# A Fourier mixing and long convolution kernel: the first transform stage with 64 points, high and low halves in one operand

## The chip, the cores and the metric

The kernel runs on one core of one Trainium2 chip, as one launch. The metric is the device time in microseconds; three runs of the kernel before gave 1201.86, 1202.92 and 1202.91, a median of 1202.91. All other times below are microseconds of one profiled execution, counted from the start of its span, unless they are marked ns.

The engines are called as the profile calls them: PE multiplies matrices (PEld is its loading of the stationary operand), DVE is the vector engine, ACT the scalar engine, POOL the GpSimd engine, and SP issues DMAs. ACT and POOL issue DMAs too.

## The reference

Four layers work on `x`, of 2048 positions (S) by 576 channels (D), all in float32. Layers 1 and 3 are A, layers 2 and 4 are B:

```
A:  n = layernorm(x)
    a = n @ Wre.T ; b = n @ Wim.T            # 576 x 576 cosine and sine matrices
    x = x + Cre @ a - Cim @ b                # 2048 x 2048 cosine and sine matrices
B:  kv = causal_conv4(k, shift_k) * v        # per channel, 4 taps
    y  = irfft(rfft(pad(kv)) * rfft(pad(ssm_k)))[:2048] + kv * ssm_D
    x  = x + layernorm(x) * y
```

B's `y` depends only on inputs, so the kernel computes it once and uses it in both B layers.

## The kernel before, in words

**Numbers.** PE multiplies in a float32 form of reduced precision. Each operand is therefore split into a high part, rounded to that form by an ACT copy, and a low part, the remainder, which DVE subtracts (`split`, line 90). A product of two split operands takes three PE products: high x high, high x low, low x high.

**First layer.** `layer` (line 291) goes through 4 column blocks x 2 matrices (Cre, Cim) x 16 row blocks: 128 steps, n = 0 to 127. A step loads a 128x512 block of C two steps ahead (`load_c`, line 204) and splits it, and issues 12 products of 512 columns into four banks `s` and two into the bank `rm`. The sixteen normed row tiles of `x` are made during the first steps (`get_x0`). At n = 15, 31, 47, ... the banks are copied out and split into `u`. After each second time, the product with W is due: 4 x 2 pieces of 27 products of 288 columns (`hidden`, line 267, bank `bk`), kept in `pending` and issued by `finish`. W (9 chunks of 128x576, split) lies in the region `ra`, which the convolution uses before.

**The branch.** Beside these steps runs the generator `branch` (line 338), which computes `y` as a transform in stages. Position s = 16p + j has p on the partitions and j = 0 to 15 as the row. There are 32 rows: 16 of the kernel `ssm_k` (src 1) and 16 of the signal kv (src 0).

- The first transform stage makes, for each row, a product over p with cosine and sine constants (`fc`, a 128 x 4 x 128 tile, loaded by POOL's queue). `f1_split` splits the row into `xf`; `f1_products` (line 423) issues for each half of the channels and each of two components three products into a bank, copies it out on ACT (`so`) and stores it to DRAM (`t_d`) from ACT's queue. Each `yield` in it ends one half of the channels, here called a group: six products before.
- Signal rows come from `convolve` (line 373), seven DVE operations for each pair of rows (1152 elements on 128 partitions), into the ring `rp` of two pairs in region `ra`, times `v`.
- The middle stage (lines 457 to 607, from `m1`) reads `t_d` back in 64 loads, makes the second transform step, the product of the two spectra, and the first inverse step; the second inverse step (`i2_products`) follows and gives `yb_d`.

**What sets the order.** The loop at line 734 interleaves steps and branch. `used` counts the calls of the branch in the first transform stage (68 at its end); `want` is a function of n and says how many should have been made; it reaches 68 at n = `F1_END` = 42. A product of a row follows its split by one or two rows. From n = `W_FROM` = 41, each half step loads one chunk of W through a ring `wl` of three tiles and splits it. At n = `MID_LOAD` = 44 the middle stage begins to load, and from `MID_FROM` = 47 its work is spread evenly over the planned time up to `I2_END` = 111, so that `spent` follows `passed`. At n = 47 all eight pieces of the first column block are issued ahead of that step's products, with middle work between them. The scheduler that places the instructions keeps each engine's queue in order at run time; `issue_after` places an instruction behind another one of the same engine.

```
want = int(4 + F1_16 * at / 8 if at <= 16 else at16 + (68 - at16) * (at - 16) / (F1_END - 16))
todo = [(1, 1), (0, 1)] + [(j, 1) for j in range(2, K_FIRST)] + [(j, 0) for j in range(K_FIRST)]
todo += [(j, src) for j in range(K_FIRST, J) for src in range(2)]
```

So before, `todo` starts with four kernel rows and four signal rows, and then alternates.

Of the kernel before, what the change touches and what calls it, by code (L numbers as in the profile page):

```python
# [15 lines left out]
P = 128  # L16
# [16 lines left out]
F1_END = 42  # L33
W_FROM = 41
HOLD = 125
W_SAVE = 60
MID_LOAD = 44
MID_FROM = 47
# [26 lines left out]
def fnet_h3_kernel(ctx: ExitStack, tc: tile.TileContext, x, c_mat, w_re, w_im, k_pad, v, shift_k,  # L65
# [126 lines left out]
    t_d = [dr.tile([P, J, 2, 2, HD], F32, name=f"t{h}") for h in range(2)]  # L192
# [22 lines left out]

    def load_w():
        lay(flts, SC_AT + CRAW * NT + 4 * D, ("wl", D, 3))
        wg = region_a(FR, "w").rearrange("p (k n) -> p k n", k=9)
        for ch in range(9):
            w = two(wg[:, ch])  # L220
            raw = ring["wl"]()
            if ch < 8:
                nc.sync.dma_start(raw, (w_re if ch < 4 else w_im)[(ch % 4) * P:(ch % 4 + 1) * P, :])
            else:
                nc.sync.dma_start(raw[:REM], w_re[NC * P:, :])
                nc.sync.dma_start(raw[REM:], w_im[NC * P:, :])
            for lo, hi, sg in ((0, P, 1 if ch < 4 else -1),) if ch < 8 else ((0, REM, 1), (REM, P, -1)):
                if sg > 0:
                    split(w[lo:hi, 0, :], w[lo:hi, 1, :], raw[lo:hi])
                else:  # L230
                    nc.scalar.activation(w[lo:hi, 0, :], raw[lo:hi], AF.Copy, scale=-1.0)
                    nc.vector.scalar_tensor_tensor(w[lo:hi, 1, :], raw[lo:hi], -1.0,  # L232
                                                   w[lo:hi, 0, :].bitcast(F32), op0=OP.mult,
                                                   op1=OP.subtract)
            W.append(w)
            yield
# [101 lines left out]
    def branch():  # L338
        f1r = region_b(FR, "f1r")
# [17 lines left out]
        def load_k(upto):  # L357
            while k_loaded[0] < min(upto, (J + 4) // 2):
# [4 lines left out]
                                          ap=[[J * D, P], [1, 2 * D]]))  # L363
# [26 lines left out]
        todo = [(1, 1), (0, 1)] + [(j, 1) for j in range(2, K_FIRST)] + [(j, 0) for j in range(K_FIRST)]  # L390
        todo += [(j, src) for j in range(K_FIRST, J) for src in range(2)]
        loads = [0]

        def f1_loads(upto):
            while loads[0] < min(upto, len(todo)):
                j, src = todo[loads[0]]
                loads[0] += 1
                if j not in fcs:
                    fcs[j] = quads(ring["fc"]())
# [11 lines left out]
        def f1_split(j, src):  # L411
# [303 lines left out]
    with tc.issue_after(biased[0]):  # L715
# [4 lines left out]
        with behind(rounded[0]):  # L720
            load_c((0, 0, 1))
        load_x(2)
    used = 4
    first_lo = parted[1]
    next(br)
    next(br)
    with behind(first_lo):
# [378 lines left out]
```

## Time and profile before

| what | before |
|---|---|
| median of three runs | 1202.91 |
| profiled execution: its time, its span | 1201.11, 1199.3 |
| PE busy, share of the span | 1180.6, 98% |
| DVE busy, share | 839.9, 70% |
| ACT busy, share | 665.9, 56% |
| granted PE clock | 0.998 |
| first-stage products (`bk<-f1r`) | 384 |

A line of a group of instructions reads: line of the kernel, engine, operation, written tile <- read tiles, shape, xcount | busy time, mean ns of one | idle time of the engine just before, and what ended it. A timeline line begins with the start and the length. Tile names: `f1r` holds `xf` and `fc`, `f1f` the convolution, `mats` the split rows of `x` and blocks of C, `flts` the loaded data, `w` the split W, `t` and `vd` the DRAM tiles between the stages, `mid` the operands of the middle stage. Matmuls overlap, so the mean of one is longer than the distance between two. A table of windows gives for each stretch the busy time of every engine in it with its count of instructions, the granted PE clock, the mean busy share of the 16 DMA engines and what they moved.

### The profile page before, as it was taken

The page shows a single profiled execution, that of the slowest core. Times are in us where ns is not written, and L with a number is a line of the kernel's source. Part 1 is how long each engine was busy: PE and PEld are TensorE (multiplying, and loading weights), DVE is VectorE, ACT ScalarE, POOL GpSimd, SP SyncE. Part 2 cuts the span into 40 slices and gives each one's busy share as a digit, 9 for nine tenths or more (in the row PEclk, how much of TensorE's full clock was granted, in tenths as well). Part 3 has the DMA queues.
Part 4 walks back from the last instruction along what each step waited for, and adds up shares of the span by engine and source line. Part 5 has one row for each costly group of instructions (what it writes and reads, how often), then busy time and mean ns, then how long its engine had stood idle before and what let it go on. Part 6 is the DMA issues. An engine that isn't in the chain of part 4 may idle for free.

```text
span 1199.3 us, 18263 instructions
## 1 busy us (share of the span) xinstructions
PE 1180.6 (98%) x6320; PEld 1026.0 (86%) x6320; DVE 839.9 (70%) x1498; ACT 665.9 (56%) x1335; POOL 75.5 (6%) x116
## 2 busy tenths in 40 slices
PE   7999999999999999999999999999999999999997
PEld 6888888988888888888988898888888888789997
DVE  7899883679777677675447766875676777774674
ACT  8855665679877768675435666544444435450210
POOL 2210000000000000001101121000000000001111
PEclk9999999999999999999999999999999999999999
DMA  9879898546656766658967686872772677794621
GB/s 340 308 226 318 275 304 256 177 133 182 216 177 199 213 180 207 187 149 249 305 202 236 222 257 213 271 264 71 216 281 74 207 275 269 237 347 142 214 96 40
DMA packets 146111, 261.96 MB, mean 218 GB/s; under 512 B 15841, under 2 KB 44769, under 8 KB 146018
## 3 DMA queue, kind: packets, MB, share of 16 engines
q1 hardware_dynamic: 102674, 205.58, 53.6%
q10 hardware_dynamic: 36432, 42.63, 10.3%
q0 software_dynamic: 6912, 12.59, 4.1%
q8 instruction: 49, 0.80, 0.3%
q14 instruction: 44, 0.36, 0.1%
HBM read 194.09 MB, written 66.65 MB: 217 GB/s over the span
## 4 chain that ended last, share of the span: by engine, by line
PE 84%; DVE 6%; DMA 4%; ACT 3%; issue 2%; POOL 1%; SPq 0%; POOLq 0%; DVEq 0%; ACTq 0%
PE s L74 46%; PE bk L74 33%; PE rm L74 5%; DMA flts<-in_c_mat 2%; ACT flts L486 1%; DVE mats L92 1%; DVE f1f L382 1%; DMA flts<-t 1%; POOL flts L616 1%; DVE mats L189 1%; ACT mid L486 1%; DVE f1f L387 0%; DMA t<-flts 0%; DVE u L92 0%; ACT mats L91 0%
## 5 line engine op out<-in xcount | busy, mean ns | idle before, releaser
L74 PE MATMUL s<-mats 128*128 128x512 f32 x2088 | 531.2, 392 | 0.8 <-DVE flts L613 0.3
L74 PEld LDWEIGHTS s<-mats 128*128 128x128 f32 x2088 | 381.1, 188 | 71.1 <-DVE mats L189 1.1
L92 DVE TENSOR_TENSOR mats<-flts,mats 128x512 fp32r<-128x512 f32 x206 | 140.7, 688 | 58.4 <-ACT mats L91 55.7
L91 ACT ACTIVATE mats<-flts 128x512 fp32r<-128x512 f32 x206 | 128.2, 627 | 85.4 <-PE bk L74 30.9
L74 PE MATMUL bk<-mid 128*128 128x288 f32 x768 | 131.1, 300 | 1.8 <-ACT flts L486 0.8
L74 PEld LDWEIGHTS bk<-mid 128*128 128x128 f32 x768 | 114.3, 188 | 21.2 <-ACT flts L486 8.4
L492 DVE TENSOR_TENSOR mid<-flts,mid 128x576 fp32r<-128x576 f32 (+1 forms) x160 | 101.9, 637 | 34.4 <-ACT mid L486 31.3
L74 PE MATMUL bk<-w,u 128*128 128x288 f32 x864 | 121.0, 296 | 0.7 <-DVE w L232 0.5
L74 PEld LDWEIGHTS bk<-w,u 128*128 128x128 f32 x864 | 117.4, 188 | 4.4 <-ACT flts L486 1.1
L486 ACT ACTIVATE flts<-bk 128x288 f32<-128x288 f32 x160 | 61.9, 404 | 87.4 <-PE bk L74 74.0
L74 PE MATMUL rm<-mats 128*128 128x512 f32 x304 | 94.9, 391 | 0.0
L486 ACT ACTIVATE mid<-flts 128x576 fp32r<-128x576 f32 (+1 forms) x159 | 86.8, 582 | 7.5 <-DMA flts<-t 3.7
L486 ACT ACTIVATE flts<-flts 64x288 f32<-64x288 f32 x192 | 85.0, 443 | 5.7
L432 ACT ACTIVATE flts<-bk 128x288 f32<-128x288 f32 x128 | 49.4, 408 | 47.0 <-PE bk L74 46.4
L74 PEld LDWEIGHTS bk<-f1r 128*128 128x128 f32 x384 | 59.5, 191 | 13.8 <-ACT f1r L91 7.4
L74 PE MATMUL bk<-f1r 128*128 128x288 f32 x384 | 64.5, 300 | 6.7 <-ACT f1r L91 6.7
L74 PE MATMUL bk<-mats 128*128 128x288 f32 (+1 forms) x376 | 67.8, 317 | 0.0
L74 PEld LDWEIGHTS rm<-mats 128*128 128x128 f32 x304 | 57.0, 188 | 12.1 <-DVE flts L264 0.3
L74 PE MATMUL s<-t,mats 128*128 128x512 f32 x264 | 64.9, 389 | 0.0
L278 DVE TENSOR_TENSOR flts<-flts,bk 128x288 f32<-128x288 f32 x48 | 21.7, 453 | 61.1 <-PE bk L74 58.8
L175 POOL TENSOR_TENSOR flts<-flts 128x1 f32<-128x1 f32 x35 | 28.9, 827 | 524.2 <-DVE flts L174 524.2
L74 PE MATMUL bk<-mats,t 128*128 128x288 f32 (+1 forms) x368 | 59.3, 303 | 0.0
(143 smaller groups left out, 1491.8 us busy)
## 6 DMA issues: line engine op xcount, KB each, us to landing
flts<-in_c_mat SPq DMA_DIRECT2D x148, 256.0 KB, 3.6
ph<-in_c_mat SPq DMA_DIRECT2D x54, 512.0 KB, 3.9
t<-flts ACTq DMA_DIRECT2D x64, 288.0 KB, 4.6
flts<-t SPq DMA_DIRECT2D x64, 288.0 KB, 2.9
flts<-in_c_mat SPq DMA_DIRECT2D x30, 512.0 KB, 5.3
vd<-flts ACTq DMA_DIRECT2D x64, 144.0 KB, 2.5
flts<-vd SPq DMA_DIRECT2D x32, 288.0 KB, 4.8
mid<-in_i2c POOLq DMA_DIRECT2D x32, 256.0 KB, 5.6
```

What stands on the lines that cost most here:

```text
L74: nc.tensor.matmul(ps, lhsT, rhs, start=first, stop=last, skip_group_check=more)
L91: a = nc.scalar.activation(h, src, AF.Copy).ins
L92: return a, nc.vector.tensor_tensor(l, src, h.bitcast(F32), OP.subtract).ins
L175: pows.append(nc.gpsimd.tensor_tensor(rs, ve, mhalf, OP.pow).ins)
L189: made.append(nc.vector.tensor_tensor(t[:, D + REM:], y[:, :NC * P], h[:, :NC * P], OP.subtract).ins)
L278: added[:] = [nc.vector.tensor_tensor(r[:, cs], r[:, cs], ps[:, :HD], OP.add).ins]
L382: nc.vector.tensor_tensor(out_t[:, n], k, wt[3 - t][:, n], OP.mult)
L432: stored[:] = [nc.scalar.activation(so[:, c, :], ps[:, :HD], AF.Copy).ins]
L486: last_act.append(nc.scalar.activation(*args, **kw).ins)
L492: nc.vector.tensor_tensor(l, src, h.bitcast(F32), OP.subtract)
L616: pows.append(nc.gpsimd.tensor_tensor(rs, sv, mhalf, OP.pow).ins)
```

## The change

The first stage's transform over 128 points becomes one over 64 points; the rows' positions are split by even and odd, and the second step becomes one of 32 points in place of 16 (constants only; the middle stage's instructions stay). The host puts the even half on partitions 0 to 63 and the odd half on 64 to 127. With 64 points, an operand's high part takes 64 partitions and its low part the other 64, so that one product covers both: `xf[0]` holds the even half's high and low parts, `xf[1]` the odd half's. A bank now takes two products (constants' high part, constants' low part), a group four.

To place the parts:
- a kernel row gets two ACT copies on 64 partitions (of the very first row, one is DVE's) and two DVE subtractions on 64 partitions that write the other half of the partitions;
- a signal row gets one ACT copy on 128 partitions, one on 64, one DVE subtraction on 128 in place, and two DMAs from SBUF to SBUF on SP's queue, each of 64 partitions x 576 elements, one call later (`crossing`).

The order `todo` becomes four kernel rows, all sixteen signal rows, then twelve kernel rows (j = 11 to 15, then 10 down to 4); some constants `fc` are loaded a second time. The calls of the branch follow a new curve: 10 at n = 14, 26 at n = 30, 43 at n = 45, and the rest by n = 49, of which 12 during the eight pieces at n = 47. The middle stage begins to load at n = 50 and runs from 53 to 111. The nine chunks of W are copied inside DRAM to `w_d` at n = 22, 24, ... 38, loaded into their final place in region `ra` at n = 45 (four) and 45.5 (five), and split in place at n = 46. At n = 46 one tile each of the rings `so` and `land` is given to the residual loads of `hidden`.

```
-F1_END = 42
-W_FROM = 41
+F1_V = 45
+F1_END = 49
+F1_PIECE = 1.5
+W_RAW = 22
+W_AT = {45: 4, 45.5: 5}
+W_SPLIT = 46
+RES_AT = 46
-MID_LOAD = 44
-MID_FROM = 47
+MID_LOAD = 50
+MID_FROM = 53
...
+    def split_raw(t, ch):
+
+        for lo, hi, sg in ((0, P, 1 if ch < 4 else -1),) if ch < 8 else ((0, REM, 1), (REM, P, -1)):
+            h, l = t[lo:hi, 0, :], t[lo:hi, 1, :]
+            if sg > 0:
+                split_in(h, l)
+            else:
+                raw = l.bitcast(F32)
+                nc.scalar.activation(h, raw, AF.Copy, scale=-1.0)
+                nc.vector.scalar_tensor_tensor(l, raw, -1.0, h.bitcast(F32), op0=OP.mult, op1=OP.subtract)
+
     def load_w():
-        lay(flts, SC_AT + CRAW * NT + 4 * D, ("wl", D, 3))
+        for ch in range(9):
+            if ch < 8:
+                load_after(w_d[ch][:, :D], (w_re if ch < 4 else w_im)[(ch % 4) * P:(ch % 4 + 1) * P, :])
+            else:
+                load_after(w_d[ch][:REM, :D], w_re[NC * P:, :])
+                load_after(w_d[ch][REM:, :D], w_im[NC * P:, :])
+            yield
         wg = region_a(FR, "w").rearrange("p (k n) -> p k n", k=9)
         for ch in range(9):
             w = two(wg[:, ch])
-            raw = ring["wl"]()
...
+            load_after(w[:, 1, :].bitcast(F32), w_d[ch][:, :D])
             W.append(w)
+            yield
+        for ch in range(9):
+            split_raw(W[ch], ch)
             yield
...
-        todo = [(1, 1), (0, 1)] + [(j, 1) for j in range(2, K_FIRST)] + [(j, 0) for j in range(K_FIRST)]
-        todo += [(j, src) for j in range(K_FIRST, J) for src in range(2)]
-        loads = [0]
+        first, last = [1, 0, *range(2, K_FIRST)], [*range(J - 5, J), *range(J - 6, K_FIRST - 1, -1)]
+        todo = [(j, 1) for j in first] + [(j, 0) for j in range(J)] + [(j, 1) for j in last]
+        loads, fc_at, crossing = [0], {}, []
...
             xf = parts("xf")
-            parted[:] = split(xf[0], xf[1], r)
+            if not src:
+                h = [nc.scalar.activation(xf[0], r, AF.Copy).ins, nc.scalar.activation(xf[1][hi], r[hi], AF.Copy).ins]
+                parted[:] = h + [nc.vector.tensor_tensor(r.bitcast(FR), r, xf[0].bitcast(F32), OP.subtract).ins]
+                crossing.extend(((xf[0][hi], r[lo]), (xf[1][lo], r[hi])))
+                return xf
+            sides = (xf[0], lo, hi), (xf[1], hi, lo)
+            if (j, src) == todo[0]:
+                h = [nc.scalar.activation(xf[0][lo], r[lo], AF.Copy).ins, nc.vector.tensor_copy(xf[1][hi], r[hi]).ins]
+            else:
+                h = [nc.scalar.activation(t[at], r[at], AF.Copy).ins for t, at, to in sides]
+            with behind(h[1]):
+                parted[:] = h + [nc.vector.tensor_tensor(t[to], r[at], t[at].bitcast(F32), OP.subtract).ins
+                                 for t, at, to in sides]
             return xf
...
-                for c in range(2):
+                for h in range(2):
                     ps = bank()
-                    mm(ps[:, :HD], fc[:, c, :], xf[0][:, cs], True, False)
-                    mm(ps[:, :HD], fc[:, c, :], xf[1][:, cs], False, False)
-                    mm(ps[:, :HD], fc[:, 2 + c, :], xf[0][:, cs], False, True)
-                    stored[:] = [nc.scalar.activation(so[:, c, :], ps[:, :HD], AF.Copy).ins]
-                nc.scalar.dma_start(t_d[hf][:, j, :, src, :], so)
+                    mm(ps[:, :HD], fc[:, 2 * h, :], xf[h][:, cs], True, False)
+                    mm(ps[:, :HD], fc[:, 2 * h + 1, :], xf[h][:, cs], False, True)
+                    stored[:] = [nc.scalar.activation(so[:, h, :], ps[:, :HD], AF.Copy).ins]
+                nc.scalar.dma_start(t_d[hf][:, :, j, src, :], so)
                 yield
...
             for half in range(2):
+                while half and crossing:
+                    dst, t = crossing.pop(0)
+                    nc.sync.dma_start(dst.bitcast(F32), t)
                 next(products, 0)
...
+    def f1_want(at):
+        return np.interp(at, (0, 14, 16, 30, 32, F1_V, F1_END), (4, 10, 11, 26, 27, 43, 68 - 2 * TB * F1_PIECE))
+
     spent = passed = 0.0
-    total = (I2_END + 1 - MID_FROM) * STEP + 3 * 2 * TB * PIECE
+    pieces = 0
+    total = (I2_END + 1 - MID_FROM) * STEP + 2 * 2 * TB * PIECE
...
+            if whole is None:
+                at, pieces = n - 0.75, pieces + 1
+            want = int(f1_want(at) + pieces * F1_PIECE)
             with behind(made[min(n + 2, J - 1)], *evac):
-                while used < want:
+                while used < min(want, 68):
                     next(br)
                     used += 1
```

More of the change, by code (lines that the diff above doesn't have):

```diff
@@ L1067, in _constants @@
         i1[1, a, :, a, :, 1] = c.T
+    r = np.arange(2 * J)
+    th = 2 * np.pi * (r[:, None] * (r // J + r % J * 2)[None, :] % 32) / 32
+    f2 = np.zeros((2, 2, 2 * J, 2, 2, 2 * J))
+    c, s = np.cos(th), np.sin(th)
+    for a in range(2):
+        f2[a, 0, :, 0, a, :] = c
+        f2[a, 1, :, 0, a, :] = s
+        f2[a, 0, :, 1, a, :] = -s
+        f2[a, 1, :, 1, a, :] = c
     m = [*_parts(f2.reshape(P, P)), *_parts(i1.reshape(P, P))]
```

90 lines of the change are left out of this document (40 added, 50 removed).

## The prediction

> **What bounds the kernel now.** I read the page first (busy shares, then the chain that ended last), next a table of windows cut at the ends of steps, and then the instruction rows of the stages that the change touches. A step is one pass of the first layer over one 128x512 block of the sequence matrix: 12 products into `s` and 2 into `rm`, so every second `rm` product ends a step.
>
> The page's busy line for all engines and its chain by engine:
> ```profile
> PE 1180.6 (98%) x6320; PEld 1026.0 (86%) x6320; DVE 839.9 (70%) x1498; ACT 665.9 (56%) x1335; POOL 75.5 (6%) x116
> PE 84%; DVE 6%; DMA 4%; ACT 3%; issue 2%; POOL 1%; SPq 0%; POOLq 0%; DVEq 0%; ACTq 0%
> ```
> The windows end at steps 0, 16, 42, 46, 52, 64, 79, 111 and at the end. Columns: stretch, length, busy of PE, PEld, DVE, ACT, POOL with instruction counts, granted clock, DMA share, GB/s.
> ```profile
> core 0: us, PE busy (x) PEld busy (x) DVE busy (x) ACT busy (x) POOL busy (x), PEclk, DMA share, GB/s
> 0.00:13.42 13.42, 6.86 (x28) 5.94 (x28) 7.91 (x26) 9.00 (x16) 2.87 (x9) 1.00 0.89 304
> 13.42:74.01 60.59, 60.15 (x282) 49.43 (x282) 53.39 (x120) 50.50 (x104) 15.00 (x17) 1.00 0.86 294
> 74.01:198.99 124.98, 124.80 (x669) 108.36 (x669) 104.39 (x123) 74.05 (x165) 5.28 (x10) 1.00 0.90 284
> 198.99:213.29 14.30, 14.30 (x71) 12.10 (x70) 4.99 (x8) 7.08 (x13) 1.58 (x3) 1.00 1.01 313
> 213.29:281.03 67.74, 66.22 (x417) 59.18 (x416) 51.48 (x102) 49.27 (x107) 0.00 (x0) 1.00 0.50 150
> 281.03:333.85 52.82, 52.82 (x277) 45.70 (x277) 44.59 (x87) 46.42 (x99) 0.00 (x0) 1.00 0.61 191
> 333.85:442.85 109.00, 108.49 (x635) 94.59 (x635) 76.36 (x153) 75.43 (x169) 2.12 (x4) 1.00 0.66 198
> 442.85:622.32 179.47, 178.69 (x1004) 156.58 (x1004) 108.27 (x197) 110.87 (x235) 13.73 (x26) 1.00 0.70 216
> 622.32:1199.30 576.98, 568.23 (x2952) 494.19 (x2951) 388.57 (x690) 243.29 (x433) 34.87 (x48) 1.00 0.63 207
> ```
> PE is busy almost everywhere, at a granted clock of 1.00. Busy can still hide a slow PE, so I take the pace of its products from a stretch in which nothing waits:
> ```profile
> 189.99 1.54 PE L74 MATMUL s<-mats 128*128 128x512 f32 x6
> 191.36 0.96 PE L74 MATMUL bk<-f1r 128*128 128x288 f32 x6
> 192.17 1.55 PE L74 MATMUL s<-mats 128*128 128x512 f32 x6
> ```
> From start to start, six 512-column products take 1.37 (0.228 each, 3.18 for the 14 of a step) and six 288-column products take 0.81 (0.135 each). Window 3 holds 26 steps, that is 364 wide products and 305 narrow ones: 364 x 0.228 + 305 x 0.135 = 124.2 of its 124.98. So PE sets the pace there, and a product that is taken out is time, as long as nothing else becomes the pace.
>
> Much else is nearly there already. In the middle of the first transform stage DVE is never idle and the DMA engines are full:
> ```profile
> 97.12:141.27 44.15, 44.15 (x243) 38.77 (x242) 43.60 (x48) 25.96 (x58) 2.64 (x5) 1.00 1.00 329
> ```
>
> **The change part by part.** *Fewer products.* `f1_products` issued 2 halves x 2 components x 3 products for each of 32 rows, 384 in all; it now issues 2 x 2 x 2, 256. 128 x 0.135 = 17.3 off PE. Shapes, banks (128), evictions (128) and stores to `t` (64) stay the same.
>
> *Start.* The first kernel row is the first thing PE uses:
> ```profile
> 5.82 0.68 ACT L91 ACTIVATE f1r<-flts 128x576 fp32r<-128x576 f32 x1 [0.75 <-DMA flts<-in_ssm_k]
> 6.54 0.76 DVE L92 TENSOR_TENSOR f1r<-flts,f1r 128x576 fp32r<-128x576 f32 x1 [0.56 <-ACT f1r L91]
> ```
> It now needs two subtractions on 64 partitions in place of one on 128, before DVE goes on to the first halves of C. A half costs no less than a whole, as ACT and then DVE rows from steps 56 to 62 show (mean ns after the comma):
> ```profile
> L486 ACT ACTIVATE flts<-flts 64x288 f32<-64x288 f32 x21 | 9.3, 443 | 0.5
> L486 ACT ACTIVATE flts<-bk 128x288 f32<-128x288 f32 x13 | 5.3, 410 | 2.4 <-ACT flts L486 1.8 <-DVE flts L508 0.5
> L506 DVE TENSOR_TENSOR flts<-bk,flts 64x288 f32<-64x288 f32 x7 | 3.2, 460 | 0.2
> L505 DVE TENSOR_TENSOR flts<-bk,flts 128x288 f32<-128x288 f32 x7 | 3.2, 457 | 5.8 <-ACT flts L486 5.8
> ```
> So one more 0.7 in the opening chain; and of the products removed here about four (0.5) only filled a wait. Cost 1.2; bounds 0.5 and 2.
>
> *Steps 1 to 16.* I count from the code which calls of the branch each step makes. Product groups (one call, now four products) done by step 16 fall from 12 to 9, convolution operations from 18 to 13; ACT gains one 64-partition copy for each of three kernel rows and loses three groups' evictions. I book no further cost.
>
> *Steps 17 to 42.* Signal rows come first, so the whole convolution must end by step 40. The calls of these steps hold 26 product groups, 14 signal rows and 43 convolution operations. DVE's pace, start to start:
> ```profile
> 99.45 1.35 DVE L382 TENSOR_TENSOR f1f<-f1f 128x1152 f32<-128x1152 f32 x1
> 100.72 0.68 DVE L92 TENSOR_TENSOR mats<-flts,mats 128x512 fp32r<-128x512 f32 x1
> 101.32 0.75 DVE L92 TENSOR_TENSOR f1r<-flts,f1r 128x576 fp32r<-128x576 f32 x1
> 101.99 1.35 DVE L387 TENSOR_TENSOR f1f<-f1f 128x1152 f32<-128x1152 f32 x1
> ```
> That is 1.27 for a convolution operation, 0.60 for a half of C, 0.67 for a row. DVE: 43 x 1.27 + 26 x 0.60 + 14 x 2 x 0.67 + 3.7 for the eviction at step 31 = 92.7. PE: 26 x 3.18 + 26 x 4 x 0.135 = 96.7. DMA, in MB: a signal row moves 0.295 (v) + 0.262 (its constants) + 0.590 (two stores) + 0.295 (k) + 0.295 (the two new crossing transfers, 64 partitions x 2304 B each) = 1.74; 13.5 rows, 26 blocks of C at 0.262 and the nine new copies of W inside DRAM (2.65) make 32.9 MB. At the 329 GB/s of the row above that is 100.0, more than PE's 96.7; there DMA was at that share and PE still lost nothing, with peaks above the mean. I take 100, a loss of 3.3 against today's 0.8: cost 2.5. Bounds: a gain of 0.8 if all losses go, and 15.6 at the slowest rate that a full stretch shows, 291 GB/s (113.1):
> ```profile
> 90.00:100.00 10.00, 10.00 (x54) 8.40 (x53) 10.00 (x13) 5.72 (x13) 0.53 (x1) 1.00 0.97 291
> ```
> ACT gets a third pass over each signal row (14 x 0.59) and has room: 74.05 of 124.98 today.
>
> *SP.* It gets 32 crossing issues, 9 copies, and 9 loads where there were 10: about 40 more at 0.33 each. They are cheap, but a crossing transfer waits for DVE's subtraction with the next load of C queued behind it. SP already waits so for buffers that a row's split frees (total, times, longest):
> ```profile
> SPq L407 <- DVE f1r L92: 14.5, 9, 4.6
> ```
> C is loaded two steps ahead, some 7.4, against a 4 to 5 landing, so I book nothing; if that cover goes, each late block costs 1 to 2. The convolution's next write of a row pair also has to wait until its crossing transfers have read it; in DVE's order about 7 of other work lies between, against 4 to 5 for issue and landing.
>
> *W.* Before, W came through three buffers from step 41 on, one chunk each half step. Now nine loads (2.65 MB) go out at steps 45 and 45.5 and nine splits (9 x 0.6 on ACT, 9 x 0.7 on DVE) are traced at step 46, ahead of the hidden products of step 47, which need all nine chunks within their first 3.6. SP, which runs about 1.5 steps ahead, issues them some 13 before they are needed. In those 13 also go three blocks of C and about six product groups' stores, loads and constants, 4.2 MB: 6.9 MB at 329 GB/s is 21, so 8 late. Filling PE meanwhile are the remaining product groups, of which 22 (12 us of PE) are traced from step 47 on. I take half, 4. Bounds: 2 better than today (window 5 today loses 1.5 idle, and a little busy), and 10.
>
> *Middle stage.* It starts at step 53 in place of 47 and still ends at 111, without the eight hidden products of step 47 beside it. The planner's total falls from 65 x 3.2 + 24 x 3.6 = 294 to 59 x 3.2 + 16 x 3.6 = 246, so 1.195 times the work in each step. Today a step of 4.38 holds one unit of nine products:
> ```profile
> 295.05:325.48 30.43, 30.43 (x160) 26.23 (x160) 24.07 (x48) 26.04 (x56) 0.00 (x0) 1.00 0.64 202
> ```
> Seven steps, seven units: a unit is about 3.0 of ACT and 2.75 of DVE. After: PE 3.18 + 1.195 x 1.21 = 4.63, ACT 0.6 + 1.195 x 3.0 = 4.2, DVE 3.9. PE stays the longest, with 91% ACT. In steps 65 to 79 (635 products: 210 x 0.228 + 425 x 0.135 = 105.3 of 109.0) 3.7 is lost today; I take 2.3 more over the stage. Bounds 0 and 6.
>
> *Sum*, on the profiled execution (span 1199.3, its time 1201.1): -17.3 + 1.2 + 2.5 + 4 + 2.3 = -7.3, so 1193.8. The median of the runs, 1202.9, lies 1.8 above that execution: 1195.6.
>
> **The rivals.** *The saving arrives almost whole.* For it: PE kept its pace at a DMA share of 1.00 and with DVE full. Then only the start and 1 us elsewhere cost: 1202.9 - 15 = 1188. *DMA becomes the pace of steps 17 to 42.* The crossing transfers are on 64 partitions, and after the first stage such transfers landed no sooner than twice the bytes did (KB each, us to landing, 199 to 218):
> ```profile
> flts<-in_w_im SPq DMA_DIRECT2D x3, 288.0 KB, 4.3
> flts<-in_w_re SPq DMA_DIRECT2D x1, 144.0 KB, 6.0
> ```
> If the 28 crossing transfers of the stage take the engines for twice their bytes, 37.0 MB at 329 GB/s is 112.6, another 12.6: 1208, slower than before. It decides from 107.3 up (100 + 7.3), that is below 307 GB/s for the plain bytes. Against it: that landing includes waiting behind others, and the two of a pair run opposite ways. [...] *W is late by its whole 8 and more*, with ACT's splits holding up the halves of C behind them: at the bound of 10, 1201.6, no change. *The products don't get fewer* is excluded by the code. *ACT sets the middle stage*: at the bound of 6, 1199.3, still faster.
>
> **How the numbers follow.** What can be told from no change here is 0.2%, 2.4 us. Forecast (with the middle stage's case) 0.52, own range 1190 to 1200; saving almost whole 0.18; DMA the pace 0.20, of which slower 0.15 and no change 0.05; W late 0.10, half no change, half slower through both. Faster 0.70, same 0.10, slower 0.20. The range for 8 in 10 leaves out the upper part of the DMA case and the lowest of the first rival: 1187 to 1208.
>
> **What would show it.** 256 products on `f1r`; a first layer in which steps 17 to 42 take about 100, with DMA share near 1.0 and DVE above 90%; waits of `s` products for halves of C if SP or DMA is late; an idle PE just ahead of the first `bk<-w,u` product if W is; ACT about 91% in steps 53 to 64. The prediction is wrong if the 26 steps take over 105, or if PE waits over 8 at step 47.

## The result, and the profile after

The change made the kernel slower: a median of 1230.53 in four runs (1227.2 to 1231.26) against 1202.91, a ratio of 1.0226 (95% interval 1.0206 to 1.0246). The prediction said 1195.6, with a range of 1187 to 1208, and faster. The profiled execution of the changed kernel took 1230.05, with a span of 1228.3 and a mean granted clock of 0.987.

The page of the changed kernel, its busy line, its chain by engine, and the group of the first-stage products:
```profile
PE 1183.6 (96%) x6192; PEld 1018.3 (83%) x6192; DVE 855.3 (70%) x1515; ACT 686.6 (56%) x1366; POOL 76.3 (6%) x123
PE 76%; ACT 7%; DMA 7%; DVE 5%; issue 3%; POOL 0%; ACTq 0%; SPq 0%; POOLq 0%; DVEq 0%
L79 PE MATMUL bk<-f1r 128*128 128x288 f32 x256 | 51.5, 321 | 20.6 <-DVE f1r L447 8.4
```
There are 128 products fewer, as said, and yet PE is busy for 3 longer: busy hides slow products. The chain has less of PE (76% against 84%) and more of ACT, DMA and issue: PE now stands waiting.

The windows of the changed kernel, cut at the ends of the same steps as those of before (0, 16, 42, 46, 52, 64, 79, 111, end), with the same columns:
```profile
0.00:18.02 18.02, 9.02 (x22) 6.44 (x22) 10.11 (x28) 11.00 (x19) 4.44 (x10) 1.00 0.86 295
18.02:80.85 62.83, 58.63 (x255) 47.26 (x256) 53.42 (x120) 50.57 (x102) 10.20 (x15) 0.97 0.78 255
80.85:188.34 107.49, 99.48 (x464) 82.18 (x464) 94.46 (x106) 54.57 (x109) 5.83 (x11) 0.97 0.90 280
188.34:207.06 18.72, 16.90 (x82) 13.58 (x82) 10.45 (x16) 13.76 (x29) 0.00 (x0) 1.00 0.93 301
207.06:282.72 75.66, 68.99 (x397) 62.43 (x397) 30.55 (x46) 40.03 (x85) 5.30 (x10) 0.91 0.69 219
282.72:341.63 58.91, 55.88 (x279) 46.70 (x279) 47.52 (x93) 49.88 (x108) 0.00 (x0) 0.97 0.66 210
341.63:456.58 114.95, 114.66 (x676) 100.15 (x676) 92.27 (x186) 90.26 (x205) 0.54 (x1) 1.00 0.64 192
456.58:651.08 194.50, 191.19 (x1076) 165.66 (x1075) 127.58 (x236) 132.67 (x283) 15.37 (x29) 1.00 0.74 225
651.08:1228.30 577.22, 568.88 (x2952) 493.85 (x2951) 388.91 (x690) 243.84 (x433) 34.66 (x48) 0.99 0.63 207
```
The last row is 577.2 long, against 577.0 before, so nearly the whole difference lies in steps 0 to 111 of the first layer, which end at 651.08 against 622.32: 28.8 later.

To see where, I take from the length of each stretch the time that its products need at PE's pace: 0.227 for one of 512 columns (14 in a step) and 0.1345 for one of 288 (the rows of the kernel before from 189.99 to 192.17 give 0.228 and 0.135). What is left I call PE's loss. Steps 17 to 42 of the changed kernel hold 364 + 100 products: 107.5 - 82.6 - 13.5 = 11.4 (11.7 with the products counted step by step, as in the table). "e1" is the first experiment below.

| steps | loss before | loss after | difference | the prediction's term | loss in e1 |
|---|---|---|---|---|---|
| 0 | 8.6 | 13.8 | +5.2 | +1.2 (start) | 13.2 |
| 1 to 16 | 2.1 | 8.0 | +5.9 | 0 | 6.3 |
| 17 to 42 | 1.7 | 11.7 | +10.0 | +2.5 | 2.3 |
| 43 to 52 | 4.4 | 17.4 | +13.0 | +4 (W) | 15.0 |
| 53 to 111 | 7.9 | 19.7 | +11.8 | +2.3 (middle stage) | 20.3 |
| sum | 24.7 | 70.6 | +45.9 | +10.0 | 57.1 |
| products at the pace | 597.5 | 580.2 | -17.3 | -17.3 | 580.2 |

So the 17.3 came, and 45.9 of losses came with it, in every stage. The loss of steps 17 to 42 isn't spread out: 8.8 of it is in step 32, 0.9 in steps 17 to 31 and 2.0 after. Step 16 alone lost 4.3. After steps 15 and 31 the banks `s` are copied out; rows of the timeline of the changed kernel around step 32 (start, length, ..., idle time before and its releaser):
```profile
128.71 0.75 DVE L438 TENSOR_TENSOR f1f<-f1f,f1r 128x576 fp32r<-128x576 f32 x1
129.38 1.35 DVE L395 TENSOR_TENSOR f1f<-f1f 128x1152 f32<-128x1152 f32 x1
129.52 1.12 SPq L476 DMA_DIRECT2D f1r<-f1f  x2
...
136.73 2.63 DVE L395 TENSOR_TENSOR f1f<-f1f 128x1152 f32<-128x1152 f32 x2 [3.33 <-DMA f1r<-f1f]
...
143.08 2.48 DVE L97 TENSOR_TENSOR u<-s,u 128x512 fp32r<-128x512 f32 x4
143.82 4.61 PE L79 MATMUL s<-mats 128*128 128x512 f32 x12 [6.31 <-DVE u L97]
```
A signal row's subtraction (L438) ends at 129.46. Its two crossing transfers are issued from 129.52 on, the second at 130.09. The convolution wants to write that row of the ring again at 133.40; it has to wait until 136.73, 6.6 after the second issue. In DVE's queue stand behind it the rest of the convolution's work and then the four subtractions that free the banks: PE waits 6.31 for the first. And when it goes on, its 12 products take 4.61, where a row of 12 takes 2.9 at the full clock (2.88 at 80.69 in the same trace). The next rows, of windows 3.4 long, say why (after the stretch its length and PE's busy time; the third number from the end is the clock):
```profile
137.00:140.40 3.40, 0.51 (x4) 0.27 (x3) 3.40 (x4) 2.37 (x5) 0.00 (x0) 1.00 0.42 138
140.40:143.80 3.40, 0.00 (x0) 0.00 (x0) 3.40 (x5) 0.00 (x0) 0.00 (x0) 0.51 0.83 253
143.80:147.20 3.40, 3.38 (x8) 2.71 (x9) 3.31 (x6) 0.86 (x2) 0.00 (x0) 0.50 0.00 1
```
In the second and the third of them the granted clock is half, 0.51 and 0.50.

The convolution waited so four times, as the table of waits of the changed kernel has it (engine, line, waited for: sum, times, longest), and this one of them stood ahead of PE's banks:
```profile
DVE f1f L395 <- DMA f1r<-f1f: 7.4, 4, 3.3
```

### The profile page after: what moved, and what is told of

Read it like the earlier page. It is cut to its first block, busy times and chain, and to the rows that moved or that the text cites. A ratio compares the mean times of both kernels' runs of the same rounds, so it can differ in the third digit from the quotient of the medians.

```text
span 1228.3 us, 18204 instructions
## 1 busy us (share of the span) xinstructions
PE 1183.6 (96%) x6192; PEld 1018.3 (83%) x6192; DVE 855.3 (70%) x1515; ACT 686.6 (56%) x1366; POOL 76.3 (6%) x123
## 4 chain that ended last, share of the span: by engine, by line
PE 76%; ACT 7%; DMA 7%; DVE 5%; issue 3%; POOL 0%; ACTq 0%; SPq 0%; POOLq 0%; DVEq 0%
PE s L79 43%; PE bk L79 29%; PE rm L79 4%; ACT flts L515 3%; DMA f1r<-f1f 2%; ACT mid L515 1%; DMA flts<-t 1%; DMA t<-flts 1%; DMA flts<-vd 1%; DVE mats L97 1%; ACT mats L96 1%; DVE mid L521 1%; DMA t<-ud 1%; DMA vd<-flts 0%; DVE f1f L395 0%
## 5 line engine op out<-in xcount | busy, mean ns | idle before, releaser
L79 PE MATMUL s<-mats 128*128 128x512 f32 x2088 | 538.9, 396 | 10.0 <-DVE u L97 7.1
L79 PEld LDWEIGHTS s<-mats 128*128 128x128 f32 x2088 | 387.1, 190 | 85.1 <-DVE u L97 8.8
L79 PE MATMUL bk<-mid 128*128 128x288 f32 x768 | 135.1, 303 | 5.7 <-ACT mid L517 2.2
L521 DVE TENSOR_TENSOR mid<-flts,mid 128x576 fp32r<-128x576 f32 (+1 forms) x160 | 102.0, 638 | 35.1 <-ACT mid L515 25.7
L515 ACT ACTIVATE flts<-bk 128x288 f32<-128x288 f32 x160 | 61.2, 402 | 67.1 <-PE bk L79 55.1
L79 PE MATMUL bk<-f1r 128*128 128x288 f32 x256 | 51.5, 321 | 20.6 <-DVE f1r L447 8.4
L459 ACT ACTIVATE flts<-bk 128x288 f32<-128x288 f32 x128 | 46.2, 406 | 44.2 <-PE bk L79 38.7
L79 PEld LDWEIGHTS bk<-f1r 128*128 128x128 f32 x256 | 42.7, 201 | 31.0 <-ACT flts L459 9.6
```

Of the source, the lines that this page charges most:

```text
L79: nc.tensor.matmul(ps, lhsT, rhs, start=first, stop=last, skip_group_check=more)
L459: stored[:] = [nc.scalar.activation(so[:, h, :], ps[:, :HD], AF.Copy).ins]
L515: last_act.append(nc.scalar.activation(*args, **kw).ins)
L521: nc.vector.tensor_tensor(l, src, h.bitcast(F32), OP.subtract)
```

## The experiments

A ratio is to the kernel before on the same chip (medians of before there: 1201.0 to 1202.2), with its 95% interval.

**The crossing by ACT, not by DMA (e1_act_cross).** Undoes the two transfers of a signal row alone; ACT copies the same halves at the same place.
```
-                    nc.sync.dma_start(dst.bitcast(F32), t)
+                    nc.scalar.activation(dst, t, AF.Copy)
```


> The changed kernel, but the two transfers per signal row that carry parts across the partition halves are two ACT copies on 64 partitions instead of DMAs from SBUF to SBUF. Theory C (the late landings of these transfers hold the convolution's next write, and with it the evacuations of steps 15 and 31 behind it on DVE): steps 16 and 32, which lose 4.3 and 8.8 us of PE in the changed kernel, lose under 3 together, and the time falls by 8 to 12, to 1219 to 1222 us. Rival O (the order on DVE, which holds convolution operations ahead of these evacuations, is enough by itself): of the 13.1 us at least 8 stay, 1225 to 1228.

Measured: 1215.94 (1215.34 to 1218.79), ratio 1.0124 (1.0109 to 1.0139): 14.9 above the kernel before, where the change is 27.6 above it. Steps 17 to 42, and the place of step 32:
```profile
78.60:176.60 98.00, 96.48 (x465) 81.30 (x464) 97.23 (x111) 73.43 (x138) 5.83 (x11) 1.00 0.87 270
134.80 2.47 DVE L97 TENSOR_TENSOR u<-s,u 128x512 fp32r<-128x512 f32 x4
135.53 3.03 PE L79 MATMUL s<-mats 128*128 128x512 f32 x12 [1.52 <-DVE u L97]
```
The 26 steps take 98.0 in place of 107.5, although ACT has 29 more instructions in them (138 against 109) and DVE is busy 97.2 of 98.0. PE waits 1.52, not 6.31, and the clock stays whole. Steps 16 and 32 lose 3.8 where the changed kernel loses 13.1, so theory C holds, though its "under 3" was too low, and the time fell by a little more than its 8 to 12: the crossing transfers cost about 13 of the 27.6.

**The crossing's bytes without anyone waiting (e7_act_traffic).** As e1, and in addition a transfer of as many bytes (64 rows of 2304 B, DRAM to DRAM) for each crossing transfer taken away, which nothing waits for.
```
+                    load_after(idle_d[len(crossing)], v[:64, j, :])
```


> The changed kernel with ACT copies in place of the crossing transfers, and at the same places of SP's queue two DMAs of the same bytes (64 rows of 2304 bytes) from DRAM to DRAM on which nothing waits. Theory C (what cost was the wait for the crossing transfers): within 2 us of 1216. Rival B, the predicted one (the bytes and the issues fill the DMA engines and the queue): 1222 to 1230, near the changed kernel.

Measured: 1217.6 (1216.54 to 1218.56), ratio 1.0122 (1.0106 to 1.0138), the same as e1. DMA issues (KB each, median from issue to landing) of the changed kernel in steps 17 to 42, and of e7 in steps 1 to 42:
```profile
f1r<-f1f SPq DMA_DIRECT2D x26, 144.0 KB, 4.8
```
```profile
idle<-in_v SPq DMA_DIRECT2D x32, 144.0 KB, 4.7
```
The bytes, the issues and the landing time are about equal; only the waiting differs. So it was the waits that cost, as theory C said, not the load on the DMA engines. (Transfers between two places of SBUF that nothing waits for were not tried.)

**The 64-point operands in the order of before (e4_before_64pt).** The kernel before with the new operands, constants and layout (crossing by ACT), but its own `todo`, calls of the branch, W and middle stage. In `f1_products`:
```
-                for c in range(2):
+                for h in range(2):
...
-                    mm(ps[:, :HD], fc[:, 2 + c, :], xf[0][:, cs], False, True)
+                    mm(ps[:, :HD], fc[:, 2 * h + 1, :], xf[h][:, cs], False, True)
```


> The kernel before, with its order, its loading of W and its middle stage, but with the 64-point operands and two products per bank; a signal row's parts are carried across by ACT copies. Theory P (the products pay where nothing is moved): 17.2 us of PE less, some of it lost to the added DVE pass of kernel rows in the stretch where DVE is full: 1188 to 1197 us. Rival D (DVE and ACT are full there, and their added passes, 16 x 0.67 and 32 to 48 x 0.59, take the whole saving): 1200 to 1208.

Measured: 1233.19 (1230.32 to 1235.21), ratio 1.0257 (1.0236 to 1.0279), beyond what any theory gave. Windows of steps 17 to 31, 32, and 33 to 42, and two of its waits in them:
```profile
80.60:157.80 77.20, 68.67 (x309) 54.15 (x308) 69.25 (x77) 55.16 (x107) 3.71 (x7) 0.96 0.78 245
157.80:174.00 16.20, 10.95 (x35) 8.19 (x35) 10.32 (x15) 12.26 (x25) 1.06 (x2) 0.68 0.65 198
174.00:224.00 50.00, 45.95 (x217) 37.32 (x217) 32.51 (x40) 39.19 (x77) 0.53 (x1) 0.97 0.67 216
```
```profile
ACT flts L444 <- DMA t<-flts: 11.8, 6, 4.1
PE bk L74 <- ACT flts L444: 9.4, 7, 1.9
```
These steps lose 35.1, against 1.7 in the kernel before. As I read it, each step is shorter with fewer products, while DVE's and ACT's work and the stores of `t` stay: evictions stand waiting for stores, PE for evictions (9.4 of the 16.8 that it waits there), and the clock falls to 0.68 of full in step 32. No run takes these apart. So the new order, with the W and the middle stage that go with it, is not what makes the change slow: with the crossing by ACT in both, the kernel with it (e1) is 17 faster than this one.

**An earlier start (e6_act_start).** As e1, with the last two calls of the branch ahead of the loop placed behind the rounding of the first row of `x`.
```
-    next(br)
-    next(br)
+    with behind(rounded[0]):
+        next(br)
+        next(br)
```


> The changed kernel with ACT copies in place of the crossing transfers, and the second kernel row's split and the first evictions held on ACT behind the first normed row. Theory S (the start, which ends step 0 4 to 5 us later than before, lost it because ACT splits a second kernel row ahead of the first row of x): step 0 ends at 14 to 15.5 instead of 17.5, the time falls by 2 to 3, 1213 to 1214 us. Rival (the added subtraction and the later landing did it): under 1 us.

Measured: 1216.24 (1213.27 to 1217.13), ratio 1.0107 (1.0087 to 1.0127): no change in time that can be told from e1. Step 0 ends at 15.8, not 17.5 (theory S said 14 to 15.5), and step 42 is still 1.5 ahead, but steps 43 to 53 lose 4.4 more (22.2 against 17.8). The earlier start didn't help here, where a later stage gave it back.

**Residual rows loaded earlier (e2_res43, e5_act_res43).** The eight pieces with W at step 47 add rows of `x`, loaded from step 46 on into one tile of `so` and one of `land`. They now come from step 43 on; e5 has e1's crossing too.
```
-RES_AT = 46
+RES_AT = 43
```


> The changed kernel, but the two tiles for the residual rows of the hidden products are taken from the other rings at step 43 instead of 46. Theory R (the residual row of the first piece is loaded late because its tile waits for a kernel row that is split behind W; PE idles 3 us and then runs cold): the wait of PE for the addition on DVE goes, 1224 to 1227 us. Rival: something else of that stage (W's splits, the evictions of the first stage) ends last right behind it, gain under 1.5, 1229 to 1231.

> The changed kernel with ACT copies in place of the crossing transfers, and the two residual tiles taken at step 43 instead of 46. Where no crossing transfer is in the way, theory R says that the 2 us wait for the residual row at step 47 goes and, if the wait was what brought the half clock, 1.7 more: 1210 to 1213 us against 1216. Rival: as with the transfers in place, it gives under 1.5.

Measured: e2 1228.26 (1226.67 to 1229.47), ratio 1.0221 (1.0206 to 1.0236); e5 1217.09 (1215.99 to 1218.53), ratio 1.0119 (1.01 to 1.0138). No gain in either. In e2 the loss of steps 48 to 50 falls from 14.6 to 9.2, and that of 43 to 46 rises from 2.8 to 6.7; in e5 they go from 14.0 to 11.6 and from 0.3 to 5.0. In e5 an eviction of the first stage waits 5.9 in steps 43 to 46 for the store that frees its tile, and PE waits 3.0 for evictions: the tiles are then missing to the first stage. In e2 PE waits 3.7 there for crossing transfers.

**No product groups among the pieces (e9_f1_off_pieces).** As e1, but the remaining groups are spread to step 52, none of them added for a piece, and the middle stage is loaded at 53 and begins at 56.
```
-F1_END = 49
-F1_PIECE = 1.5
+F1_END = 52
+F1_PIECE = 0
...
-MID_LOAD = 50
-MID_FROM = 53
+MID_LOAD = 53
+MID_FROM = 56
```


> The changed kernel with ACT copies in place of the crossing transfers, and the rest of the first transform stage spread over steps 45 to 52 with none of it between the eight pieces of step 47; the middle stage starts three steps later, at 56. Theory F (the first stage's groups among the pieces and W's splits ahead of them on ACT cost the 17 us that PE loses in steps 43 to 53): the loss from step 43 to the first middle work, step 56, falls to under 10, that of the middle stage rises by 1 to 2 from 17.5; 1208 to 1212 us. Rival W (W's nine loads and splits and the late residual row alone hold the pieces): the loss stays at 15 or more; 1216 to 1220.

Measured: 1223.44 (1222.42 to 1224.82), ratio 1.0184 (1.0169 to 1.0199), 6 to 7 slower than e1. Steps 48 to 50 do lose less without the groups, 10.2 against 14.0, but steps 51 to 55 lose 8.6 more, 13.3 against 4.7. So the groups among the pieces account for some 4 of the 17.8, and theory F, which had the loss up to step 56 under 10 (it is 24.4), falls. One of its waits from 190 to 290, that is from step 46 on:
```profile
ACT flts L459 <- DMA t<-flts: 13.2, 9, 2.8
```
From step 46 on `so` has three tiles, not four, and evictions wait for the stores that free them.

**No residual loads, four tiles for stores (e12_act_no_residual).** As e1, without the residual loads of those eight pieces (a stale tile is added in their place), so that `so` keeps its four tiles.
```
-            (spare_so, *so), (spare, *land) = ([ring[name]() for _ in ring[name].tiles] for name in ("so", "land"))
-            ring["so"], ring["land"], ring["res"] = Ring(so), Ring(land), Ring([spare_so, spare])
+            spare, *land = [ring["land"]() for _ in ring["land"].tiles]
+            ring["land"], ring["res"] = Ring(land), Ring([spare])
```


> As e1_act_cross, but the eight loads of the residual rows for the pieces with W at step 47 are left out (a stale tile is added, so the output is not the reference's), the pieces use one tile that the landing ring gives, and the store ring keeps its four tiles instead of three. In e1 PE loses 17.8 in steps 43 to 53; the rows there show a wait of 2.0 for a late residual row and evictions that wait for stores of t, beside a wait of 2.3 for evictions that stand behind the nine splits of W on ACT. Theory S, that late residuals and the shorter store ring are most of it: loss of steps 43 to 53 falls to 10 to 12, time 1208 to 1211. Rival W, that the nine splits on ACT ahead of the evictions, and the half clock that follows, are most of it: the 2.3 wait and its half-clock stretch stay at the first piece, loss stays at 15 to 18, time 1213 to 1217.

Measured: 1212.88 (1210.93 to 1214.93), ratio 1.0096 (1.0079 to 1.0113). Steps 43 to 53 lose 13.4 where e1 loses 17.8: between the two theories, some 3 to 4 for the residual rows and the shorter ring. What stays, first in e1, then here:
```profile
199.76 0.53 PE L79 MATMUL bk<-f1r 128*128 128x288 f32 x2 [2.28 <-ACT flts L459]
200.36 5.37 PE L79 MATMUL bk<-w,u 128*128 128x288 f32 x27
```
```profile
197.41 0.68 ACT L229 ACTIVATE w<-w 64x576 fp32r<-64x576 f32 x1
198.12 1.39 ACT L446 ACTIVATE f1r<-flts 64x576 fp32r<-64x576 f32 x2
199.99 0.66 PE L79 MATMUL bk<-f1r 128*128 128x288 f32 x2 [2.23 <-ACT flts L460]
```
ACT's evictions stand in its queue behind the last splits of W (the last ends at 198.1) and the split of a kernel row; PE waits 2.2 for them, in both, and in e1 the first piece then takes 5.37 where a piece takes 3.7.

**The denser middle stage, in the kernel before (e3_before_mid53).** The kernel before, with its middle stage from step 53 to 111 and the pieces of step 47 without it.
```
-MID_FROM = 47
+MID_FROM = 53
...
-    total = (I2_END + 1 - MID_FROM) * STEP + 3 * 2 * TB * PIECE
+    total = (I2_END + 1 - MID_FROM) * STEP + 2 * 2 * TB * PIECE
...
+        if whole is None and n < MID_FROM:
+            finish(pending, 1)
```


> The kernel before, with the middle stage's work spread over steps 53 to 111 instead of 47 to 111; nothing else is moved. Theory M (the denser middle stage costs about what the changed kernel loses more there, 8 us): 1209 to 1214 us. Rival (as predicted, PE stays the longest and only 2 to 3 are lost): 1204 to 1207.

Measured: 1206.31 (1204.92 to 1208.66), ratio 1.0041 (1.0028 to 1.0055). Steps 54 to 111 lose 15.8, against 7.9 in the kernel before and 15.9 in the changed one. So the added loss of 8 in these steps comes with the later begin alone, as theory M said. Here the stage ahead of it gives some back, as it has the pieces to itself (steps 43 to 53 lose 0.6, against 4.3 before): 5.3 slower in all, which is why the time lies in the rival's range.

**Less work for ACT in the middle stage (e10_mid53_less_act, e11_before_less_act).** e3 and the kernel before, both with two of the small ACT copies of each middle unit left out, so that the spectra's product takes another operand; nothing else is changed.
```
-            act(kk[hi, 1, :], kk[hi, 0, :], AF.Copy, scale=-1.0)
-            act(kk[hi, 0, :], kk[lo, 0, :], AF.Copy)
...
-            nc.vector.tensor_tensor(p2[lo], px[hi, :HD], kk[hi, 1, :], OP.mult)
+            nc.vector.tensor_tensor(p2[lo], px[hi, :HD], kk[hi, 0, :], OP.mult)
```


> The kernel before with the middle work spread over steps 53 to 111 (1206 us), and two of the four small ACT copies of each middle unit left out, so that the product of the two spectra is computed from wrong operands (64 x 2 copies of 64x288, 0.44 us each). Theory A (in the denser middle stage ACT, in its fixed order, is what PE waits for): of the 15.8 us that PE loses in steps 54 to 111 at least 7 go, so this kernel comes below 1199 and gains clearly more than the next one does. Rival (PE and the banks themselves, or DVE, set it): the loss falls by no more than in the next kernel.

> The kernel before with the same two copies of each middle unit left out (the product of the spectra is wrong in the same way), as the measure for the run before this one. Theory A: PE loses 7.9 us in steps 54 to 111 of the kernel before, of which 3 to 4 go, 1197 to 1200 us. Rival: within 1.5 of the kernel before.

Measured: e10 1197.6 (1196.87 to 1200.25), ratio 0.9965 (0.9954 to 0.9975), 8.7 below e3 (9.8 when each is set against the kernel before on its own chip); e11 1196.82 (1194.75 to 1197.31), ratio 0.9957 (0.994 to 0.9974), 5.3 below the kernel before. Steps 54 to 111, in order: before, e11, e3, e10:
```profile
286.60:622.32 335.72, 334.44 (x1882) 291.91 (x1881) 224.03 (x425) 227.40 (x490) 15.85 (x30) 1.00 0.67 207
```
```profile
286.90:618.90 332.00, 331.54 (x1881) 292.60 (x1880) 221.67 (x421) 184.28 (x388) 15.85 (x30) 1.00 0.67 209
```
```profile
266.60:627.40 360.80, 356.26 (x2010) 308.47 (x2010) 264.17 (x509) 268.49 (x587) 15.90 (x30) 1.00 0.67 209
```
```profile
265.30:620.00 354.70, 352.06 (x2011) 308.37 (x2010) 261.40 (x509) 213.71 (x459) 15.84 (x30) 1.00 0.69 212
```
The products are the same in each pair. With 55 of ACT's time taken out, the denser stage is 6.1 shorter; with 43 out, that of before is 3.7 shorter. In time, the difference between the dense and the loose stage shrinks from 5.3 to 0.8. A fifth of ACT's work taken out takes 39% of the loss in the dense order (15.8 to 9.6, so 6.2, a little short of theory A's 7) and 46% in the other (7.9 to 4.3), although ACT is busy for only 74% and 68% of the stretch. So ACT's part of a unit is a large part of what PE loses in the middle stage; whether by its load or by the length of the unit's chain, which the copies lengthen too, these runs don't tell apart, nor what the rest is.

**Waits put into the kernel before (e8_before_holds).** 5, 8 and 12 extra DVE operations on the first bank, ahead of the copying out at steps 31, 63 and 95.
```
+                        nc.vector.tensor_tensor(ring["rt"](), ps[0], xs[:, 0, :NT].bitcast(F32), OP.mult)
```


> The kernel before, with 5, 8 and 12 added DVE operations of 512 columns on the first bank ahead of the evacuations of steps 31, 63 and 95, so that PE waits at the next step; the results are the same. Theory K (a wait of PE beyond some 2 us is followed by a stretch of half clock, as at steps 16 and 32 of the changed kernel): each such wait is followed by 3.4 us or more at a granted clock of 0.5, and the loss at that step is the wait and half of that stretch; with waits of about 1, 3 and 5 us the time rises by 12 to 15, to 1213 to 1216 us. Rival (a wait costs itself): 8 to 10, 1209 to 1211 us.

Measured: 1208.73 (1206.56 to 1210.25), ratio 1.0049 (1.0031 to 1.0066), less than either theory gave. The only longer waits of PE that came of it are 2.47 and 1.12, since other products were placed into the rest. The window with the 2.47, and the next:
```profile
520.70:524.10 3.40, 1.56 (x7) 0.94 (x6) 2.63 (x5) 0.74 (x2) 0.00 (x0) 1.00 0.10 37
524.10:527.50 3.40, 2.74 (x12) 2.01 (x12) 2.98 (x6) 0.69 (x2) 0.00 (x0) 1.00 0.02 5
```
The clock stays whole here, at 1.00 behind the wait of 2.47; the run doesn't show what the 6.31 of step 32 alone would cost.

None of these that does the kernel's whole work is faster than the kernel before; apart from e3 and e8, which keep the old operands, the nearest are e1 and its variants e5, e6 and e7, 1.1 to 1.2% above it.

## Why the prediction was wrong

*Fewer products*: right. 256 are left, and PE's time at its pace fell by the 17.3.

*Start*, "one more 0.7 in the opening chain", 1.2 with bounds 0.5 and 2: it was 5.2. The step counted DVE's second subtraction and four products. The timelines show what it left out, first a row of PE and one of ACT of the kernel before, then the changed kernel:
```profile
6.56 2.60 PE L74 MATMUL bk<-f1r 128*128 128x288 f32 x9 [6.56 <-ACT f1r L91]
7.22 0.85 ACT L182 ACTIVATE early<-early,flts 128x576 f32<-128x576 f32 x1
```
```profile
7.99 2.11 PE L79 MATMUL bk<-f1r 128*128 128x288 f32 x6 [7.99 <-DVE f1r L447]
8.58 0.68 ACT L445 ACTIVATE f1r<-flts 64x576 fp32r<-64x576 f32 x1 [0.79 <-DMA flts<-in_ssm_k]
9.29 0.87 ACT L187 ACTIVATE early<-early,flts 128x576 f32<-128x576 f32 x1
12.38 5.06 PE L79 MATMUL s<-mats 128*128 128x512 f32 x11 [0.19 <-DVE mats L97]
```
ACT splits part of the second kernel row, after a wait of 0.79 for its landing, ahead of the first row of `x`, which it took up at 7.22 before and at 9.29 now; in e6, where the first row of `x` goes first, step 0 is 1.7 shorter than in e1. PE's own begin moved from 6.56, behind ACT's rounding, to 7.99, behind DVE's second subtraction, by 1.4 where 0.7 was counted: a product that takes both parts in one operand can't begin before the low part is there. And PE's next products run at 0.46 each, half of the pace, until 17.24, where the kernel before reached its pace at about 11 (the record of the clock begins at 17.56 in this trace and at 10.41 in the one before, so the 1.00 of the tables' first rows says nothing of the time ahead of it). By the first rows of the two tables, PE's idle time is 2.4 of the 5.2 (9.0 against 6.6); the other 2.8 are products that ran slower.

*Steps 1 to 16*, "I book no further cost": 5.9, of which 4.1 is step 16. There PE waits for a crossing transfer itself, and its next 12 products take 4.25, at half clock:
```profile
74.45 0.50 PE L79 MATMUL bk<-f1r 128*128 128x288 f32 x2 [1.90 <-DMA f1r<-f1f]
```
 By e1, where step 16 loses 2.0 rather than 4.3, about half of that one is the crossing; what the other half is stays open.

*Steps 17 to 42*, "I take 100, a loss of 3.3": 107.5, over the 105 that the prediction named as its refutation. Neither DMA (a share of 0.90 at 280 GB/s) nor DVE (94.5 of 107.5) was the pace, and e1 shows that 98.0 can be had. The sums for DVE (92.7, measured 94.5) and PE (96.7, its products at the pace 96) were right; that of the bytes, from which the 100 came, was too high: 30.1 MB were moved, not 32.9, and 30.1 at the prediction's 329 GB/s take 91, less than PE's products. What failed is the sentence under *SP*: "about 7 of other work lies between against 4 to 5 for issue and landing". In step 32 it was 4.0 of work (129.38 to 133.40) against 6.6 from issue to landing. Nothing was booked for that, since the numbers used were means. Where the banks are copied out, what stands behind DVE is PE's own next step; another wait of DVE for a crossing transfer, 2.67 at 174.13, cost PE at most the 2.0 that steps 33 to 42 lose.

*DMA becomes the pace*, the rival on the slower side, would have given 1208. It falls too: steps 17 to 31 and 33 to 42, with nearly all of the stage's crossing transfers, lost 2.9 together, and e7 puts the bytes back for nothing (a ratio of 1.0122, against e1's 1.0124). That such a transfer takes the engines for twice its bytes, as the rival supposed, no run shows. The landings in steps 17 to 42 of the changed kernel, and in e7 for the middle one, were 4.8 for the 144 KB on 64 partitions, 4.7 for as many bytes inside DRAM, and 4.9 for the 288 KB of a row of `v` on 128 partitions; no run here has a transfer on 64 partitions alone.

*W*, "8 late", of which half was taken, bounds -2 and 10: 13.0, outside. The chunks of W were in time; the pieces' first products wait for none. "PE waits over 8 at step 47" did not come as one wait either. The mechanism was another: (a) the nine splits, which the prediction priced but booked no wait for, stand ahead of evictions on ACT (1.3 of waiting in the changed kernel, 2.3 and 2.2 in e1 and e12, and in these two the half clock behind it); (b) a late residual row and a store ring of three tiles, neither of which it counted (e12: 4.4 of loss, 3 to 4 of time); (c) the half clock, as here in the changed kernel:
```profile
219.25 0.45 DVE L290 TENSOR_TENSOR flts<-flts,bk 128x288 f32<-128x288 f32 x1 [3.31 <-DMA flts<-in_x]
219.76 1.33 PE L79 MATMUL bk<-f1r 128*128 128x288 f32 x4 [2.75 <-DVE flts L290]
220.88 5.93 PE L79 MATMUL bk<-w,u 128*128 128x288 f32 x27
```
In steps 43 to 53 the changed kernel loses 21.2; the waits of PE that the profile lists there come to 10.6, and the 16.5 at half clock to at most 8.2. How the rest of the 13 divides among these is not settled.

*Middle stage*, 2.3 with bounds 0 and 6: 11.8. Of it 3.8 is step 53, where ACT waits 6.5 for the stage's first load from `t`, PE 2.2 for ACT, and the clock halves for 3.4:
```profile
286.70 0.40 PE L79 MATMUL bk<-mid 128*128 128x288 f32 x1 [2.17 <-ACT mid L517]
```
The prediction had no such step. The other 8.0 are the mechanism it named, a denser stage, mis-sized: "PE stays the longest, with 91% ACT", and so little was added. ACT was busy for 85% of steps 53 to 64, where the prediction named 91%, and for 75% of steps 54 to 111, and still PE loses 15.9 in these; e10 and e11 show that much of it is to ACT. So here ACT's mean share over the stage didn't bound what PE waited for within a unit.

The sum of the five differences is 45.9, less 17.3: 28.6, against 28.8 in the traces' ends of step 111.

## What to carry to other kernels

When products are taken off the engine that sets the pace, look at each place where another engine's queue frees what that engine needs next, and compare the cover there with the longest landing, not the median with the mean. Here a hand-over between partitions inside a chain was cheaper as a copy on an engine with room than as a transfer that a full queue had to wait for, although the DMA engines had the bandwidth (e1 1.0124 and e7 1.0122 of the kernel before, the change 1.0226). A term of 2 for "a little denser" needs a row in which the stage was as dense, or an experiment that makes the old kernel as dense first.

## What the hardware showed that I had not expected

In the changed kernel's trace the record of PE's granted clock, from 17.56 on, holds 1.00 and 0.50 only. Ahead of the end it has five stretches at 0.50: from 75.59, 140.44, 218.95, 266.74 and 287.22, of 3.41, 6.83, 6.83, 6.83 and 3.41, 27.3 in all. They and the whole stretches between them (61.44, 71.68, 40.96 and 13.65) are all multiples of 3.41. The record of the kernel before is 1.00 from 10.41 to 1194.84; e1 has two stretches of half clock, 6.8 together (0.96 over its steps 43 to 53, 192.8 to 274.9). What came before them was not always an idle stretch; a thin one was enough here: after 1.52 busy of 3.40 the next stretch was at half, and after 2.54 of 3.40 it stayed there:
```profile
215.50:218.90 3.40, 1.52 (x12) 1.28 (x10) 0.45 (x1) 0.98 (x3) 0.00 (x0) 1.00 0.98 322
218.90:222.30 3.40, 2.54 (x10) 2.54 (x11) 1.80 (x3) 1.63 (x4) 0.53 (x1) 0.51 0.27 96
222.30:225.70 3.40, 3.40 (x16) 3.40 (x16) 0.75 (x1) 0.33 (x1) 0.00 (x0) 0.50 1.06 320
```
After 1.56 of 3.40 in e8 (above) it stayed whole. Busy time alone doesn't draw the line, as a row of e1 with more of it, and a half stretch behind it, shows:
```profile
251.70:255.10 3.40, 1.75 (x8) 1.19 (x8) 1.51 (x2) 3.20 (x7) 0.00 (x0) 1.00 0.46 160
```
On the grid of the changed kernel's record, the last whole stretch of 3.41 ahead of each of the five had PE busy for 1.17, 0.48, 1.48, 1.40 and 1.25; of those with a whole one behind them the least busy had 2.23 (the last row):
```profile
72.18:75.59 3.41, 1.17 (x6) 0.62 (x5) 3.41 (x6) 1.67 (x4) 0.00 (x0) 1.00 0.95 290
137.03:140.44 3.41, 0.48 (x4) 0.24 (x2) 3.41 (x4) 2.34 (x5) 0.00 (x0) 1.00 0.43 137
215.54:218.95 3.41, 1.48 (x12) 1.24 (x10) 0.41 (x1) 0.94 (x3) 0.00 (x0) 1.00 0.97 319
263.32:266.74 3.42, 1.40 (x9) 0.89 (x7) 0.34 (x1) 1.48 (x5) 0.00 (x0) 1.00 0.57 205
283.80:287.22 3.42, 1.25 (x7) 0.69 (x5) 0.54 (x1) 1.21 (x2) 0.00 (x0) 1.00 1.01 379
198.47:201.88 3.41, 2.23 (x12) 1.57 (x10) 0.40 (x1) 1.12 (x3) 0.00 (x0) 1.00 0.97 321
```
The half stretches there with PE busy for 0.04, 2.60 and 3.12 had another half one behind them, the five that were busy throughout (3.41) a whole one. Behind the wait of 2.28 in e1 (199.76) the first piece took 5.37 in place of 3.7; the 2.75 of the changed kernel (up to 219.76) ends in a half stretch of 6.83, which cost PE 3.4 at most, an estimate from its length. If PE would have been busy in all of the 27.3 but the 3.4 of step 32 in which it waited anyway, half clock took some 12 of the 45.9, an estimate from these rows.
